# Router transposes in unused columns of score tiles, q's three pieces two steps each, ScalarE's, GpSimd's and the load jobs at other steps

## The chip, the cores and the metric

The kernel runs on one core of a Trainium2 chip. The core has five engines with in-order instruction queues: TensorE (matmuls and transposes, in the profile PE, with its weight loads as PEld), VectorE (DVE), ScalarE (ACT), GpSimd (POOL) and SyncE (SP), which here only issues DMAs. Matmul results land in PSUM, eight banks; everything else is in SBUF. The metric is the device time of one execution in microseconds, lower is better.

## What is computed

Sparse attention over 4 batch entries, 8 heads, 576 positions and head size 64, then a top-1 mixture of eight experts over the 2304 tokens, then one more layer for all tokens:

```python
scores = scale * q @ k.T                      # per batch entry and head, 576 x 576
thresh = max(scores) - tau
attn = softmax(where(scores >= thresh, scores, -1e9))
x = (attn @ v) -> (2304, 512)
logits = x @ w_gate                           # the router
e = argmax(logits); gate = softmax(logits)[e]
out = gate * (relu(x @ w1[e]) @ w2[e])
h = out @ w_in; result = (h - tanh(h)) @ w_out
```

All in float32 with the accuracy of float32: the kernel splits operands into a high and a low part and adds up several matmuls.

## The kernel before

**Attention stage.** `Attn.run` works through 16 units, which this text calls heads: unit u is head u % 8 of two batch entries at once (u // 8 chooses which two). Each has nine steps t = 0 to 8, one score tile of 128 rows by 576 columns each, so there are 144 steps. In step i the program emits the score matmuls of tile i + 2 (`scores`, L228), the row maximum of tile i + 1 (`smax`, VectorE, L236), its exponential (`sexp`, ScalarE, L242), and the mask of tile i (`smask`, VectorE, L255). A step ahead of all that and behind it has four phases, 0 to 3, in which further jobs stand; the queue of each engine is in the order of emission.

**The jobs of a head.** Their places are the table `PL`: step relative to the head's first step, and phase. A head's q and k are prepared some steps before: `dq` doubles q on GpSimd (`xq`, L129), `hi1` and `lo1` split k on ScalarE and GpSimd (L120, L124), `q0`, `m`, `q4` are q's three pieces of transposes on TensorE (L175; `m` holds one block of q and one of k), `k0`, `k5` those of k (L173). Each piece goes through one PSUM bank, tag "t", one buffer; it is evacuated by ScalarE (`eq0`, `em`, `eq4`, `ek0`, `ek5`; L197, L200, L204) and for q also by a VectorE subtraction for the low part (`fq0`, `fm`, `fq4`; L208), and the next piece has to wait for both. `vw`, `vh`, `vl` scale and split v (ScalarE L146, L150; GpSimd L154); `vm` are v's maxima for four heads (VectorE L132), done in four neighbouring steps of heads 3, 7 and 11.

Behind the mask, `se` casts the weights to 16 bits (ScalarE L263, tile e16, three buffers for groups of three steps), `sl` subtracts for the low part (GpSimd L267, L268, a large one for two steps and a small one for the third), `te` has SyncE issue a DMA transpose of a group (L273), which also frees its e16 buffer. The first three blocks of each group are transposed by TensorE instead into unused columns of a score tile (`tr_m`, L284, columns 288 to 480 of its first bank) and copied by ScalarE (`ev_m`, `et`, L287). `pv` multiplies with v (L311) into a bank that it shares with the router's logits; `po0` to `po2` read it on VectorE (L317), `st` stores.

**The router in the attention stage.** After each odd head the 512-wide rows of a head pair are ready. `lg_tr` transposes nine 128 x 128 blocks, in three groups, through the "t" bank (`lps`, L563), `lg_ev` copies each group on ScalarE (`xT`, L567), `lg_mm` multiplies with the router's weights (L571), `lg_add` adds to the logits on VectorE (L580). In `PL` these are `t0` to `t2`, `v0` to `v2`, `l0` to `l2` and `la`.

**Loads.** `lq`, `lk`, `lv` load q, k and v of four heads at once from SyncE's queue (L96 to L111), in which the DMA transposes and the stores stand too. q and k share one tag with three buffers.

**Expert layers.** After the last `lg_add` all tokens are routed, sorted by expert through indirect DMAs, and the expert layers and the last layer run.

The loop's core, in its order of emission:

```python
ps[i + 2] = self.scores(*steps[i + 2], ...)
nn[i + 1] = self.smax(ps[i + 1])
ee[i + 1] = self.sexp(ps[i + 1], nn[i + 1])
self.smask(*steps[i], ps.pop(i), nn.pop(i), ee.pop(i))
```

## Time and profile before

| | us |
|---|---|
| median of 3 runs | 1070.12 |
| lowest, highest | 1066.64, 1074.0 |
| the profiled execution, its own time | 1065.54 |
| its span, first to last instruction | 1063.8 |

Busy shares of that span: TensorE 88%, its weight loads 82%, VectorE 82%, ScalarE 68%, GpSimd 56%; mean granted TensorE clock 0.96. The attention stage takes about the first third of the span, the expert layers and the last layer the rest. A share is an average over these stages. In the rows below PE, PEld, DVE, ACT, POOL and SP are the engines, L an instruction's line in the kernel, `out<-in` its tiles. A row of waits says which engine and line stood for which, how long in total, how often, and the longest. Square brackets behind a row of the timeline are the idle time of that engine before the instruction and what ended it.

### The profile page before, as it was taken

To read this page: it belongs to the slowest core of one execution; us is meant where nothing else is said; L and a number is where in the kernel's file an instruction comes from. 1 tells how busy PE (TensorE), PEld (TensorE's weight loads), DVE (VectorE), ACT (ScalarE), POOL (GpSimd) and SP (SyncE) were. 2 spreads that over 40 slices of the span, in tenths; PEclk is the share of its full clock that TensorE was granted. 3 is DMA by queue.
4 is the path that set the end of the run, shared out by engine and by line. 5 is a ranking of instruction groups with operands and counts; after the bars stand their busy time and mean duration, and the time that the engine had idled before them with its cause. 6 is when DMAs were issued, how large, how long until landed. Compare 5 with 4: busy or idle time off the path is not lost.

```text
span 1063.8 us, 20919 instructions
## 1 busy us (share of the span) xinstructions
PE 940.9 (88%) x7441; PEld 869.2 (82%) x7441; DVE 872.7 (82%) x1667; ACT 721.4 (68%) x1359; POOL 597.0 (56%) x581
## 2 busy tenths in 40 slices
PE   4577787887787498999999998999999999999997
PEld 4466676776786398999999997889999999999986
DVE  5789979888985678786777787999989889898893
ACT  4698998897995175666676766666666566556662
POOL 2788877887876211120011027786867768677763
PEclk9699988998998599999999999999999999999999
DMA  5599999998979497786898875120101001000000
GB/s 138 106 194 170 174 184 180 173 188 182 147 142 170 119 311 251 252 264 223 273 307 279 281 255 171 46 77 21 48 1 42 26 21 48 1 30 1 21 11 31
DMA packets 230826, 147.85 MB, mean 139 GB/s; under 512 B 161306, under 2 KB 207660, under 8 KB 230717
## 3 DMA queue, kind: packets, MB, share of 16 engines
q1 hardware_dynamic: 226957, 135.68, 51.2%
q0 software_dynamic: 3312, 10.49, 3.1%
q8 instruction: 60, 0.98, 0.4%
q14 instruction: 49, 0.40, 0.1%
q10 hardware_dynamic: 448, 0.30, 0.1%
HBM read 85.08 MB, written 23.60 MB: 102 GB/s over the span
## 4 chain that ended last, share of the span: by engine, by line
PE 46%; DVE 10%; DMA 5%; ACT 2%; issue 2%; another core or an unknown queue 0%; SPq 0%; POOL 0%; POOLq 0%; DVEq 0%; ACTq 0%
PE h L1054 22%; PE y L1137 15%; PE y L1109 8%; DMA raw<-in_moe_w_dram 3%; DVE w L1255 2%; DVE w L1256 2%; DMA wscr<-cm 1%; DVE w L1024 1%; DVE w L1253 1%; DVE tm L1254 1%; DVE w L1257 1%; PE t L1031 1%; ACT w L1022 0%; DVE cm L1185 0%; DVE keep L584 0%
## 5 line engine op out<-in xcount | busy, mean ns | idle before, releaser
L267 POOL TENSOR_TENSOR e<-em,e 128x1024 f16<-128x1024 f32 (+1 forms) x98 | 158.1, 1614 | 61.1 <-issue 29.9
L1252 POOL TENSOR_SCALAR tm<-u 128x384 uint8<-128x384 f32 x88 | 128.9, 1465 | 50.2 <-ACT u L1248 49.6
L1054 PE MATMUL h<-xa,w 128*128 128x256 f32 (+6 forms) x864 | 139.3, 311 | 3.3 <-DVE hbuf L1090 1.3
L1109 PE MATMUL y<-hbuf,w 128*128 128x256 f32 (+6 forms) x864 | 139.8, 310 | 0.3 <-ACT yo L1112 0.2
L1054 PEld LDWEIGHTS h<-xa,w 128*128 128x128 f32 x864 | 129.7, 193 | 5.2 <-DVE hbuf L1090 1.8
L255 DVE SCALAR_TENSOR_TENSOR em<-sps,n,e 128x576 f32<-128x576 f32 x144 | 116.8, 811 | 15.8 <-ACT et L287 4.8
L1109 PEld LDWEIGHTS y<-hbuf,w 128*128 128x128 f32 x864 | 127.4, 190 | 1.2 <-ACT yo L1112 0.8
L1248 ACT ACTIVATE u<-h 128x384 f32<-128x384 f32 x96 | 47.1, 491 | 117.5 <-PE h L1054 117.5
L242 ACT ACTIVATE e<-sps,n 128x576 f32<-128x576 f32 x144 | 108.5, 754 | 26.3 <-DVE n L236 26.1
L1255 DVE SCALAR_TENSOR_TENSOR w<-y,w 128x384 f32<-128x384 f32 x96 | 122.5, 1276 | 0.0
L1071 POOL DMA_INDIRECT xr<-rows,idx x26 | 27.3, 1049 | 163.8 <-PE t L1031 158.8
L236 DVE TENSOR_REDUCE n<-sps 128x1 f32<-128x576 f32 x144 | 107.2, 744 | 11.1 <-PE sps L228 11.1
L311 PE MATMUL ops<-vh,et 128*128 128x64 f16 (+1 forms) x2240 | 94.9, 200 | 20.7 <-DVE x L317 20.7
L1054 PE MATMUL h<-xk,w 128*128 128x384 f32 x576 | 109.2, 337 | 2.0 <-DVE w L1024 1.7
L311 PEld LDWEIGHTS <-et 128*128 128x128 f16 (+1 forms) x2240 | 84.1, 106 | 31.1 <-issue 25.7
L1054 PEld LDWEIGHTS h<-xk,w 128*128 128x128 f32 x576 | 102.1, 188 | 6.7 <-DVE w L1024 2.4
L1269 POOL TENSOR_TENSOR gl<-w,gh 128x384 fp32r<-128x384 f32 x83 | 84.6, 1019 | 38.8 <-ACT gh L1268 38.8
L228 PE MATMUL sps<-ka,qa 128*128 128x288 f32 x320 | 84.5, 356 | 19.2 <-DVE n L246 9.1
L263 ACT CAST e<-em 128x576 f16<-128x576 f32 x144 | 98.8, 687 | 3.3 <-DMA et<-e 1.2
L1024 DVE TENSOR_TENSOR w<-raw,w 128x1024 fp32r<-128x1024 f32 x68 | 84.0, 1238 | 20.6 <-ACT w L1022 19.9
L1022 ACT CAST w<-raw 128x1024 fp32r<-128x1024 f32 x72 | 75.4, 1050 | 18.7 <-DVE free L611 11.9
L1256 DVE SCALAR_TENSOR_TENSOR w<-y,w 128x384 f32<-128x384 f32 x96 | 77.7, 809 | 10.0
(237 smaller groups left out, 2207.6 us busy)
## 6 DMA issues: line engine op xcount, KB each, us to landing
raw<-in_moe_w_dram SPq DMA_DIRECT2D x64, 512.0 KB
cv<-in_moe_w_in_dram SPq DMA_DIRECT2D x16, 512.0 KB
cv<-in_moe_w_out_dram SPq DMA_DIRECT2D x16, 512.0 KB
wscr<-cm SPq DMA_DIRECT2D x32, 256.0 KB
raw<-wscr SPq DMA_DIRECT2D x16, 512.0 KB
xw<-yT SPq DMA_DIRECT2D x24, 192.0 KB
vv<-in_v_dram SPq DMA_DIRECT2D x8, 512.0 KB
raw<-in_k_dram SPq DMA_DIRECT2D x6, 512.0 KB
```

Of the source, the lines that this page charges most:

```text
L236: nc.vector.tensor_reduce(out=n[:, 0:1], in_=ps[:, :, 0:288], axis=AX.XY, op=ALU.max, negate=True)
L242: nc.scalar.activation(out=e, in_=ps[:, :, 0:288], func=AF.Exp, bias=n[:, 0:1])
L255: nc.vector.scalar_tensor_tensor(out=self.em[u, g][:, i].rearrange("p (a b) -> p a b", a=2), in0=ps[:, :, 0:288], scalar=n[:, 1:2], in1=e, ...
L263: self.nc.scalar.copy(self.e16[u, g][:, i, 0:S], self.em[u, g][:, i])
L267: eng.tensor_tensor(out=e16[:, r, S + 64:], in0=em[:, r, 0:512], in1=e16[:, r, 0:512], op=ALU.subtract)
L311: nc.tensor.matmul(o[q], lhsT=et[:, base + c, q], rhs=vh[:, a, j, c if c < 5 else c - 5, :], start=(n == 0), stop=(n == len(terms) - 1))
L1054: self.nc.tensor.matmul(out, lhsT=a, rhs=b, start=(i == 0), stop=(i == len(parts) - 1))
L1109: nc.tensor.matmul(self.ys[d], lhsT=a[:, f % 2, s], rhs=b, start=(f == 0 and i == 0), stop=(f == 7 and i == 2))
L1137: nc.tensor.matmul(self.ys[m], lhsT=a[:, s], rhs=b[:, f % 2], start=(f == 0 and i == 0), stop=(f == 15 and i == 2))
L1252: nc.gpsimd.tensor_scalar(out=mk, in0=u, scalar1=RCUT * RCUT, scalar2=None, op0=ALU.is_gt)
L1255: V.scalar_tensor_tensor(out=w, in0=y, scalar=b, in1=w, op0=ALU.add, op1=ALU.mult)
L1256: V.scalar_tensor_tensor(out=w, in0=z, scalar=d, in1=w, op0=ALU.add, op1=ALU.mult)
```

## The change

The router's transposes of six of the eight head pairs (those of heads 1, 3, 5, 7, 9 and 11) no longer go through the "t" bank: a pair of blocks is transposed into columns 288 to 416 of the two banks of a score tile, ahead of its score matmuls (`lg_tr2`, at the steps `LGS`), and copied out by ScalarE right behind that tile's exponential (`lg_ev2`). Five copies take the place of three, and the small matmuls (`lg_mm2`) stand two steps after the transposes. The pairs of heads 13 and 15 keep the former way. In `PL` q's pieces and k's now stand at even distances of two steps and one or two for k, with ScalarE's evacuations at the head of the following step; `dq`, `hi1`, `lo1`, `vw`, `vh`, `vl` and the loads `lq` and `lv` stand at other steps. The first head's own table (`PFIRST`) and the last's (`PLAST`) stay.

```diff
--- before.py
+++ after.py
@@ -27,6 +27,7 @@
 RM = S - 512
 QS = S + 64
 MLAG = 3, 4
+LGS = 22, 23, 25, 26, 28
 
 
 class Attn:
@@ -208,11 +209,13 @@
         self.nc.vector.tensor_tensor(out=self.qview(self.QB[u % 2], what), in0=self.pview(pf, what),
                                      in1=self.qview(self.QA[u % 2].bitcast(F32), what), op=ALU.subtract)
 
-    def scores(self, u, t, m=None):
+    def scores(self, u, t, m=None, l=None):
         nc = self.nc
         ps = self.sp.tile([128, 2, 512], F32, tag="s", name="sps")
         if m:
             self.tr_m(ps, *m)
+        if l:
+            l[0].lg_tr2(ps, *l[1:])
         qa, qb, ka = self.QA[u % 2], self.QB[u % 2], self.ka[u]
         if t == 4:
             terms = [(j, 512 + 64 * j) for j in range(2)]
@@ -331,10 +334,10 @@
 
     LD = (6,)
 
-    PL = {"lq": (-21, 1), "lk": (-31, 2), "lv": (-12, 1), "dq": (-15, 1), "hi1": (-15, 3),
-          "lo1": (-13, 3), "q0": (-11, 1), "eq0": (-10, 1), "fq0": (-10, 2), "m": (-10, 2), "em": (-9, 1), "fm": (-9, 3), "q4": (-9, 3),
-          "eq4": (-8, 0), "fq4": (-8, 2), "k0": (-5, 0), "ek0": (-5, 0), "k5": (-5, 2), "ek5": (-4, 0),
-          "vm": (-7, 3), "vn": (-3, 1), "vc": (-3, 2), "vw": (4, 3), "vh": (5, 3), "vl": (6, 1),
+    PL = {"lq": (-25, 1), "lk": (-31, 2), "lv": (-18, 1), "dq": (-17, 1), "hi1": (-19, 1),
+          "lo1": (-14, 1), "q0": (-12, 1), "eq0": (-11, 0), "fq0": (-11, 2), "m": (-10, 1), "em": (-9, 0), "fm": (-9, 2), "q4": (-8, 1),
+          "eq4": (-7, 0), "fq4": (-7, 2), "k0": (-6, 1), "ek0": (-5, 0), "k5": (-5, 1), "ek5": (-4, 0),
+          "vm": (-7, 3), "vn": (-3, 1), "vc": (-3, 2), "vw": (3, 0), "vh": (6, 1), "vl": (7, 1),
           "se": (1, 2), "sl": (2, 0), "te": (4, 2), "pv": (11, 3), "po0": (14, 2),
           "po1": (20, 3), "po2": (20, 3), "de": (9, 3), "rc": (13, 1), "st": (32, 3), "t0": (23, 1), "v0": (24, 1), "l0": (31, 2),
           "t1": (24, 3), "v1": (24, 3), "l1": (28, 3), "t2": (29, 0), "v2": (29, 2), "l2": (30, 1), "la": (32, 2)}
@@ -355,7 +358,7 @@
     def run(self, units, moe=None):
         nc = self.nc
         NU = len(units)
-        sched = {}
+        sched, lgs = {}, {}
         PL = self.PL
         for x in self.AFTER:
             x, y = x.split()
@@ -402,7 +405,13 @@
             at(b, "de", self.denom, u)
             at(b, "rc", self.recip, u)
             at(b, "st", self.store, u)
-            if moe and u % 2 == 1:
+            if moe and u % 2 == 1 and b + LGS[-1] + 2 < 9 * NU:
+                P, j = u // H, u % H // 2
+                for x, i in enumerate(LGS):
+                    lgs[b + i] = moe, P, j, x
+                    sched.setdefault((b + i + 2, 3), []).append((moe.lg_mm2, (P, j, x)))
+                at(b, "la", moe.lg_add, P, j)
+            elif moe and u % 2 == 1:
                 P, j = u // H, u % H // 2
                 for g in range(3):
                     at(b, f"t{g}", moe.lg_tr, P, j, g)
@@ -419,12 +428,14 @@
                 f(*a)
             if 0 <= i + 2 < len(steps):
                 j = i - MLAG[0]
-                ps[i + 2] = self.scores(*steps[i + 2], (steps[j][0], steps[j][1] // 3) if j >= 0 and j % 3 == 0 else None)
+                ps[i + 2] = self.scores(*steps[i + 2], (steps[j][0], steps[j][1] // 3) if j >= 0 and j % 3 == 0 else None, lgs.get(i))
             for f, a in sched.get((i, 1), []):
                 f(*a)
             if 0 <= i + 1 < len(steps):
                 nn[i + 1] = self.smax(ps[i + 1])
                 ee[i + 1] = self.sexp(ps[i + 1], nn[i + 1])
+            if i - 1 in lgs:
+                moe.lg_ev2(ps[i + 1], *lgs[i - 1][1:])
             j = i - MLAG[1]
             if 0 <= j < len(steps) and j % 3 == 0:
                 if i + 2 - MLAG[1] + MLAG[0] >= len(steps):
@@ -485,7 +496,7 @@
     def __init__(self, tc, at, wg, w1, w2, w_in, w_out, out, rows, yT, cp, dp):
         self.tc, self.nc, self.attn, self.ident = tc, tc.nc, at, at.ident
         self.w1, self.w2, self.out, self.xtok, self.yT = w1, w2, out, rows, yT
-        self.cp, self.dp, self.xT, self.wgd = cp, dp, {}, wg
+        self.cp, self.dp, self.xT, self.xT2, self.wgd = cp, dp, {}, {}, wg
         nc = self.nc
         self.gscr = dp.tile([NTL, 128], F32, name="gscr")
         self.wscr = dp.tile([16, 128, 1024], F32, name="wscr")
@@ -565,6 +576,20 @@
     def lg_ev(self, P, j, g):
         self.xT[g] = self.attn.wk.tile([128, 3, 128], F32, tag="xT", name="xT", bufs=3)
         self.nc.scalar.copy(self.xT[g], self.lps[:, 0:3])
+
+    def lg_tr2(self, ps, P, j, x):
+        at = self.attn
+        for i in range(min(2, 9 - 2 * x)):
+            self.nc.tensor.transpose(ps[:, i, 288:416], at.X[4 * P + j][:, 2 * x + i], at.ident)
+
+    def lg_ev2(self, ps, P, j, x):
+        n = min(2, 9 - 2 * x)
+        self.xT2[x] = self.attn.wk.tile([128, 3, 128], F32, tag="xT", name="xT", bufs=3)
+        self.nc.scalar.copy(self.xT2[x][:, 0:n], ps[:, 0:n, 288:416])
+
+    def lg_mm2(self, P, j, x):
+        for i in range(min(2, 9 - 2 * x)):
+            self.nc.tensor.matmul(self.attn.lm[:, 2 * x + i], lhsT=self.xT2[x][:, i], rhs=self.wg[:, j], start=True, stop=True)
 
     def lg_mm(self, P, j, g):
         for i in range(3):
```

## Rows read from the trace of the kernel before

**Rows 1.** The page, first line: span and instructions.

```profile
span 1063.8 us, 20919 instructions
```

**Rows 2.** Timeline, VectorE: start us, duration, engine, line, operation, [idle before, releaser].

```profile
349.94 0.23 DVE L580 TENSOR_TENSOR L<-L,ops 128x72 f32<-128x72 f32 x1 [2.71 <-PE ops L571]
```

**Rows 3.** Busy time by head: length, engines, TensorE clock, DMA; last row fourteen heads.

```profile
78.97:100.00 21.03, 15.21 (x199) 13.61 (x200) 19.72 (x52) 18.38 (x35) 17.99 (x20) 0.92 0.97 181
100.00:117.84 17.84, 15.93 (x246) 14.96 (x244) 16.53 (x45) 16.55 (x30) 13.76 (x14) 1.00 0.69 109
117.84:139.64 21.80, 15.79 (x197) 14.26 (x198) 16.50 (x44) 18.92 (x35) 18.71 (x20) 0.84 1.05 219
157.47:180.30 22.83, 16.42 (x210) 14.74 (x211) 20.14 (x52) 17.98 (x34) 17.63 (x19) 0.85 1.03 196
198.12:219.68 21.56, 16.32 (x198) 14.83 (x198) 16.66 (x44) 18.50 (x35) 17.71 (x20) 0.84 1.11 223
237.50:260.56 23.06, 16.42 (x200) 14.78 (x200) 19.87 (x52) 18.12 (x34) 18.16 (x20) 0.85 0.93 194
278.38:298.28 19.90, 14.70 (x198) 13.35 (x198) 16.51 (x44) 18.41 (x35) 17.63 (x19) 0.91 0.98 176
42.52:316.11 273.59, 216.90 (x3020) 198.89 (x3019) 241.03 (x629) 243.15 (x438) 217.78 (x219) 0.93 0.93 172
```

**Rows 4.** Timeline of head 5, 131 to 136 us: ScalarE, TensorE, VectorE.

```profile
131.42 0.67 ACT L263 CAST e<-em 128x576 f16<-128x576 f32 x1 [0.99 <-POOL e L268]
132.00 0.82 ACT L146 ACTIVATE vv<-vv,sc 128x640 f32<-128x640 f32 x1
132.73 0.67 ACT L204 ACTIVATE ka<-tps,g 128x512 fp32r<-128x512 f32 x1
133.45 0.90 PE L563 MATMUL lps<-ident,x 128*128 128x128 f32 x3 [2.40 <-ACT ka L204]
134.12 0.82 DVE L255 SCALAR_TENSOR_TENSOR em<-sps,n,e 128x576 f32<-128x576 f32 x1 [1.77 <-issue]
135.18 0.83 PE L228 MATMUL sps<-ka,qa 128*128 128x288 f32 x2
```

**Rows 5.** Waits of VectorE, heads 1 to 14: us in total, times, longest.

```profile
DVE n L236 <- PE sps L228: 9.6, 14, 1.5
DVE em L255 <- ACT et L287: 4.8, 11, 0.8
DVE pm L132 <- DMA vv<-in_v_dram: 4.8, 3, 2.4
```

**Rows 6.** Waits of TensorE, heads 1 to 14.

```profile
PE tps L175 <- DVE qb L208: 19.3, 15, 1.6
PE ops L311 <- DVE x L317: 17.0, 21, 1.4
PE lps L563 <- ACT ka L204: 7.1, 6, 2.4
```

**Rows 7.** Groups by line and shape, heads 1 to 14: busy us, mean ns.

```profile
L287 ACT COPY et<-sps 128x384 f16<-128x384 f16 x41 | 19.8, 484 | 0.0
L567 ACT COPY xT<-lps 128x384 f32<-128x384 f32 x18 | 8.7, 486 | 1.7 <-PE lps L563 1.6
L200 ACT CAST qa<-tps 128x128 fp32r<-128x128 f32 x14 | 3.6, 259 | 0.0
L208 DVE TENSOR_TENSOR qb<-tps,qa 128x512 fp32r<-128x512 f32 x28 | 19.2, 685 | 1.3 <-ACT qa L200 0.6
L132 DVE TENSOR_REDUCE pm<-vv 128x1 f32<-128x640 f32 x12 | 9.7, 812 | 4.8 <-DMA vv<-in_v_dram 4.8
```

**Rows 8.** Waits of SyncE's DMA queue, heads 1 to 14.

```profile
SPq L273 <- POOL e L268: 78.6, 24, 6.6
```

**Rows 9.** Timeline of the start: first scores; doubling of head 1's q.

```profile
14.18 0.82 PE L228 MATMUL sps<-ka,qa 128*128 128x288 f32 x2 [2.80 <-DVE ka L202]
15.43 1.14 POOL L129 COPY xq<-raw 128x1152 f32<-128x1152 f32 x1 [12.83 <-DMA raw<-in_q_dram]
```

## The prediction

> **What bounds the kernel now.** The page gives the span [rows 1]: the profiled execution took 1065.54 us by its time, 1063.8 us of it from first to last instruction. The chain of waits that ended last can be followed back only into the expert layers, which the change leaves alone; there I looked for what they start from. In the timeline the last addition of router logits ends at 350.2 us, having waited for the router's last matmul [rows 2]. The routing takes a maximum over all those logits, so everything behind it moves one to one with that instruction. What the change can move is the attention stage ahead of it.
>
> There I cut the table of engine busy time by heads, from one head's first row maximum to the next one's [rows 3]. The pattern is the main finding. Even heads last 17.84 us at a granted clock of 1.00 (heads 4, 6, 8, 10, 12 and 14 are alike within 0.02 us). Odd heads, which do the same nine steps, last 19.90 to 23.06 us at 0.84 to 0.92. Fourteen heads take 273.59 us. VectorE is busy 16.5 us in an even head and in a plain odd one (5, 9, 13); in heads 3, 7 and 11, which carry the four v maxima, 19.7 to 20.1.
>
> What is different in an odd head shows in the timeline of head 5 [rows 4]. TensorE stood 2.40 us before the router's transposes `lps`: they want the one "t" bank, which still holds a k piece, and its evacuation `ka` (L204, 132.73) stands on ScalarE behind a late cast (0.99 us) and v's scaling (L146, 132.00). The exponential is queued behind these, and the mask starts at 134.12 after 1.77 us of idle VectorE. The scores, in order behind `lps`, come only at 135.18, and their pair of matmuls takes 0.83 us. The waits over the 14 heads fit: VectorE 9.6 us for scores, 4.8 for v's load in three waits, 4.8 for the `et` copy [rows 5]; TensorE 7.1 us at `lps`, 19.3 for the evacuation of q's low parts, 17.0 for the `x` outputs [rows 6].
>
> **The change part by part.** *Router transposes in score tiles.* Six of the eight head pairs no longer take the "t" bank. Transposes and small matmuls stay nine each per pair, so TensorE gains no work; the place in the queue changes: a pair of transposes now stands directly before a tile's score matmuls, where they wait for nothing but the slot that the scores need as well. The 7.1 us wait and what hangs on it go. The evacuation becomes five copies instead of three. Three were 0.486 us each for 384 columns; a 128-column cast from the "t" bank takes 0.259 [rows 7], so I put 256 columns between, at 0.37. In the six pairs that is 24 x 0.37 + 6 x 0.26 = 10.4 us against 18 x 0.486 = 8.7: 1.7 us more on ScalarE over 14 heads, 0.1 us a head.
>
> More than their length counts where they stand: right behind the exponential, and the mask of that tile reads the same banks. Today the mask waits for the `et` copy out of its own tile in 11 cases, 4.8 us together, 0.44 each [rows 5]; there are 41 such copies in the stretch [rows 7], so about one in four holds it. The Trainium skill, page "PSUM — Partial Sum Buffer", section "PSUM bank collisions raise a hardware error", says that two engines are to be kept apart on one bank, two reads of different columns included. The trace agrees (those 11 waits); by the page the 30 new copies are all ahead of their masks, and if unused columns were really free, this term would be 0. Price from the rows: nothing if ScalarE is always early, 30 x 0.37 = 11 us if it is always late; I take one in four at 0.44: 3.0 us, nearest to the `et` rows.
>
> *q's pieces two steps apart.* Now the middle piece's transposes are queued directly behind the VectorE subtraction that frees their bank, once a head, and this is the 19.3 us [rows 6]. With a step between, the subtraction is done when TensorE gets there. TensorE is not the bound in even heads (clock 1.00, VectorE's wait for scores is small), so most of it is hidden anyway. What comes late instead: q4's subtraction now stands in the same step directly before the two `x` outputs, whose bank TensorE wants; its wait of up to 1.4 us there [rows 6] grows by about one subtraction of 512 columns, 0.685 us [rows 7]. The next scores have a step's lead, which covers that; without cover it would be 14 x 0.7 = 10 us.
>
> *ScalarE and GpSimd dealt out.* v's scaling moves from beside the two k evacuations to a step of its own, the cast of v's high part and k's split likewise. In an even head VectorE is idle 17.84 - 16.53 = 1.3 us [rows 3], and such a clump of scaling and evacuation is one cause; I take back 0.3 (bounds 0 and 1.3). On GpSimd each group of a large and a small subtraction now gets one extra job behind the small one, so the DMA transpose that SyncE issues no longer waits for it; SyncE stood 78.6 us for these subtractions [rows 8]. This costs nothing where ScalarE's next cast into the same e16 slot is still later; where it is not, I read the 0.99 us before a cast [rows 4] as such a case: the row names the subtraction that ended last, but the slot is freed only by the DMA transpose of three groups before.
>
> *Loads.* q is asked for four steps, v six steps earlier: about 8 and 12 us. The 4.8 us of v waits [rows 5] go. The q load now waits for the doubling of the last head of its group, one step before it, with DMA transposes queued behind it on SyncE; the doubling is a GpSimd copy of 1.14 us [rows 9], done while SyncE is busy with the transpose ahead; without that cover it costs SyncE 3 x 1.14 = 3.4 us, at worst all of it time.
>
> *Start.* Head 1's first q piece now stands before the first scores. They start at 14.18 us, but the doubled q is there only at 15.43 + 1.14 = 16.57 [rows 9]: up to 2.4 us plus the transposes' own. The first exponential already stands behind that piece's evacuation on ScalarE, so the mask hardly moves: between 0 and 3, I take 0.5.
>
> **The sum.** Base for a head without v maxima: 17.84 - 0.3 = 17.5. Plain odd heads: (21.80 - 17.5) + (21.56 - 17.5) + (19.90 - 17.5) = 10.8. Heads 3, 7, 11: VectorE's own work, 16.53 + 4 x 0.812 [rows 3, 7] = 19.8: 1.2 + 3.0 + 3.3 = 7.5. Even heads: 6 x 0.3 = 1.8. Together 20.1; less 3.0 for the copies and 0.5 for the start: 16.6, say 17 us. Check from below: ScalarE is busy 243.15 us in these 273.59 [rows 3], with the longer copies 244.9; so no more than 28 us can go. Against the profiled execution's own 1065.5 this is 1048.5. The runs shown have a median of 1070.1, 4.6 us above it; new runs will lie between these scales, and I forecast **1051 us**.
>
> **Rivals.** *The copies hold the masks, and ScalarE is late in odd heads* (0.18). ScalarE is busy 18.92 us in head 5 against 16.55 in head 4 [rows 3], though the code gives only two copies more, 0.97 us. If that is real work, plain odd heads stay near 18.9 and lose 3 x 1.4 = 4 us, and the copies rise towards their 11. Gain 5 to 13; at 9 it is 1059. For it: the mask's waits for `et`. Against it: the rest of the 18.92 is likely instructions that no longer overlap in a stalled queue.
>
> *The DMA transposes become the bound, no change* (0.07). Heads that follow faster ask for their e16 slots sooner. The 0.99 us wait of a cast [rows 4] would have to come 17 times, somewhat more than once a head, to eat the gain: 1068. For it: SyncE's long waits, and transposes, loads and stores on one queue. Against it: ScalarE shows such a wait in few places, and the small subtractions come sooner.
>
> *TensorE's clock, slower* (0.07). Odd heads run at 0.84 to 0.92, and in head 5 a 2.40 us stand comes before scores that take 0.83 us [rows 3, 4]. The place is the wait for the `x` outputs: 1.4 us today, 2.1 with the subtraction before it, in every head; it decides if even heads fall below 1.00 as well. Then they last like heads 13 and 5, 2.1 to 4.0 us longer: 6 x 3 = 18 us, and the odd ones gain nothing: 1065.5 + 18 = 1083. Against it: the waits at q's middle piece and at `lps` go, and each even head has had a wait of this kind at 1.00. The Trainium skill, page "TensorE: Matmul & The Clock Gate", section "A second HAM failure mode: psum-queue depth-cycling", says that short idles between groups of matmuls that cycle through PSUM can make the clock oscillate; by it the slower case would be the rule here. The even heads' 1.00 does not agree.
>
> *More than forecast* (0.06): the even heads too come down to ScalarE's floor, gain 25 to 28, 1040.
>
> **How the numbers follow.** Forecast 0.62 with 1043 to 1057: the even heads' term between 0 and 1.3 a head, the copies between 0 and 6, the start up to 3. Taking in most of the first rival, the range is 1041 to 1063; the slower case, no change and the larger gain stay outside with 0.20. A change of 1%, 10.7 us, is about what a measurement of this kernel can tell from none. Faster by more: 0.62 + 0.06 + half the first rival = 0.77; within 1%: 0.09 + 0.07 = 0.16; slower 0.07.
>
> **What would show it.** Right: odd heads without v maxima at 17.4 to 18.0 us and clock 1.00, heads 3, 7, 11 near 19.8; no wait at `lps` before head 13's; no VectorE wait for v's load; the wait for q's low part gone; the mask's wait for the router copies a few us; the last logit addition at about 333. Wrong: new waits of a mask for `xT` over 8 us, casts waiting for the DMA transposes, even heads below clock 1.00, or later layers that take longer than before.

## The result and the profile after

The changed kernel takes 1056.37 us (median of 4 runs, 1053.64 to 1057.43), the kernel before beside it 1070.86: a ratio of 0.987 with a 95% interval of 0.984 to 0.990, 14.5 us less. The forecast was 1051, its range 1041 to 1063. The profiled execution took 1053.64 us, 11.9 less than the 1065.54 of before, with this span on the page:

```profile
span 1051.9 us, 20946 instructions
```

The last addition of router logits ends 13.5 us sooner than before [rows 2]. Timeline of the changed kernel, VectorE:

```profile
336.46 0.23 DVE L605 TENSOR_TENSOR L<-L,ops 128x72 f32<-128x72 f32 x1 [2.71 <-PE ops L596]
```

Busy time by head of the changed kernel, columns as in [rows 3]: heads 2 to 5, 7, 10, 12 and 13, and the fourteen heads:

```profile
58.81:78.92 20.11, 15.27 (x203) 14.32 (x202) 16.45 (x44) 16.98 (x32) 17.24 (x19) 0.83 1.12 215
78.92:100.61 21.69, 16.59 (x219) 15.22 (x215) 19.91 (x52) 18.33 (x34) 17.92 (x19) 0.92 0.88 147
100.61:117.22 16.61, 14.74 (x238) 14.11 (x238) 16.43 (x44) 16.47 (x33) 13.63 (x15) 1.00 0.78 128
117.22:136.13 18.91, 15.66 (x227) 14.43 (x226) 16.41 (x44) 17.19 (x34) 16.14 (x17) 1.00 1.09 230
...
155.35:175.65 20.30, 15.28 (x221) 13.84 (x218) 19.85 (x52) 17.86 (x33) 16.99 (x19) 1.00 1.01 184
...
210.22:229.60 19.38, 15.21 (x211) 14.16 (x211) 16.57 (x45) 17.65 (x35) 15.89 (x17) 0.91 1.12 221
...
250.25:266.88 16.63, 14.55 (x237) 13.92 (x237) 16.38 (x45) 16.63 (x33) 14.27 (x15) 1.00 0.79 125
266.88:284.06 17.18, 14.38 (x222) 13.58 (x221) 16.42 (x45) 17.10 (x34) 16.14 (x17) 1.00 1.03 191
...
42.03:299.88 257.85, 209.97 (x3012) 196.03 (x3013) 239.40 (x628) 240.58 (x448) 217.78 (x219) 0.95 0.97 181
```

The fourteen heads lost 15.7 us. Where: heads 5, 9 and 13 together 9.2 (63.3 to 54.0 us), heads 3, 7 and 11 4.3, the even heads 4, 8, 12 and 14 5.6, head 1 1.0. Heads 2, 6 and 10 grew by 4.3 (18.71, 17.83, 17.82 to 20.11, 19.22, 19.38), which no term of the forecast's sum had. Head 12 is the picture of a head at its floor: 16.63 us long, VectorE busy 16.38 and ScalarE 16.63 of it.

Waits of the changed kernel over the same heads (columns as in [rows 5]):

```profile
PE ops L314 <- DVE x L320: 35.4, 27, 3.7
...
ACT e L266 <- DMA et<-e: 9.5, 9, 2.2
...
DVE n L239 <- PE sps L231: 3.8, 6, 1.0
...
DVE em L258 <- ACT xT L588: 1.8, 5, 0.4
...
PE tps L176 <- DVE qb L209: 0.4, 1, 0.4
```

TensorE's wait for q's low part went from 19.3 us to 0.4, that for the `x` outputs doubled from 17.0 to 35.4 [rows 6], VectorE's for scores fell from 9.6 to 3.8 [rows 5], and the waits at `lps` and for v's load are gone. New is ScalarE's: casts wait 9.5 us for DMA transposes in nine waits, in the kernel before 1.0 in two, or 2.0 with the one that its profile puts down to GpSimd [rows 4].

Outside the fourteen heads, head 1 begins 0.5 us sooner (42.03 us instead of 42.52), the part from the last row maximum to the last logit addition takes 23.48 us instead of 20.40, and all behind it 715.44 instead of 713.86. The other profiles have 713.94 to 716.11 for that last part, and 713.94 and 716.11 are two executions of one program (e3, e3b), so its 1.6 us tell nothing.

### The profile page after: what moved, and what is told of

Same layout as the page of the kernel before. It is cut to its first block, busy times and chain, and to the rows that moved or that the text cites. A ratio compares the mean times of both kernels' runs of the same rounds, so it can differ in the third digit from the quotient of the medians.

```text
span 1051.9 us, 20946 instructions
## 1 busy us (share of the span) xinstructions
PE 933.8 (89%) x7441; PEld 866.5 (82%) x7441; DVE 872.8 (83%) x1667; ACT 719.2 (68%) x1371; POOL 596.9 (57%) x581
## 4 chain that ended last, share of the span: by engine, by line
PE 47%; DVE 10%; DMA 4%; issue 3%; ACT 3%; POOL 0%; SPq 0%; POOLq 0%; DVEq 0%; another core or an unknown queue 0%; ACTq 0%
PE h L1079 23%; PE y L1162 15%; PE y L1134 8%; DVE w L1280 2%; DVE w L1281 2%; DMA raw<-in_moe_w_dram 1%; DVE w L1049 1%; DMA xr<-rows,idx 1%; DVE w L1278 1%; DMA cv<-in_moe_w_in_dram 1%; ACT w L1047 1%; DVE tm L1279 1%; PE t L1056 1%; DVE w L1282 1%; DMA wscr<-cm 1%
## 5 line engine op out<-in xcount | busy, mean ns | idle before, releaser
L245 ACT ACTIVATE e<-sps,n 128x576 f32<-128x576 f32 x144 | 110.7, 769 | 15.5 <-DVE n L239 14.9
L266 ACT CAST e<-em 128x576 f16<-128x576 f32 x144 | 101.1, 703 | 12.3 <-DMA et<-e 9.5
L1049 DVE TENSOR_TENSOR w<-raw,w 128x1024 fp32r<-128x1024 f32 x68 | 84.1, 1238 | 20.2 <-ACT w L1047 20.0
L1047 ACT CAST w<-raw 128x1024 fp32r<-128x1024 f32 x72 | 75.4, 1051 | 17.9 <-DVE free L636 12.0
```

The costliest lines, as they stand in the source:

```text
L245: nc.scalar.activation(out=e, in_=ps[:, :, 0:288], func=AF.Exp, bias=n[:, 0:1])
L266: self.nc.scalar.copy(self.e16[u, g][:, i, 0:S], self.em[u, g][:, i])
```

## The experiments

Each run is read by its time in the fourteen heads of its profile, since the rest of the program is the same. What the runs hold, and the result; the whole time is the median of as many runs as the brackets say:

| run | router in tiles | q and k spaced | jobs dealt out | q, v load at | fourteen heads, us | whole time, us (runs) |
|---|---|---|---|---|---|---|
| before | | | | -21, -12 | 273.59 | 1070.86 (4) |
| e1 | x | | | -21, -12 | 272.10 | 1066.50 (1) |
| e9 | | | v's scaling alone | -21, -12 | 265.04 | 1061.19 (1) |
| e5, e5b | | | x | -21, -12 | 260.11, 262.98 | 1054.58 (1), 1055.38 (4) |
| e8 | x | | x | -25, -18 | 273.77 | 1068.17 (1) |
| e2 | x | x | | -25, -18 | 263.40 | 1060.28 (1) |
| after; e4 | x | x | x | -25, -18 | 257.85; 260.27 | 1056.37 (4); 1057.27 (1) |
| e6; e7 | x | x | x | -21, -18 | 259.72; 263.88 | 1059.13 (8); 1060.10 (10) |
| e3, e3b | x | x | x | -21, -12 | 256.84, 257.43 | 1051.23 (1), 1053.96 (4) |
| e10 | x | x | x | -21, -14 | 251.90 | 1048.31 (4) |

The kernel before took 1062.62 us in the one run beside e1 to e4, 1067.28 (median of 17) beside e5 to e8, and 1069.51 (of 7) beside e9, e10, e3b and e5b.

e5 and e5b are one program, as are e3 and e3b, and e4 differs from the changed kernel only behind these heads. The pairs are 2.9, 0.6 and 2.4 us apart, so differences of less than 3 us between two profiles tell nothing by themselves; a single head differs by up to 2.4 us between two executions of one program (head 5: 18.35 in e3, 20.79 in e3b). q's spacing without the router in the score tiles was not tried: by the order of emission the router's transposes and q's pieces would then wait for each other at the "t" bank.

### The router alone (e1_router_alone)

```diff
 # the changed kernel, with the whole table PL of the kernel before
-    PL = {"lq": (-25, 1), ..., "vl": (7, 1), ...}
+    PL = {"lq": (-21, 1), ..., "vl": (6, 1), ...}
```

> The kernel before with only the router's transposes moved into the score tiles; all other jobs and loads stand where they stood. Measured from the first row maximum of head 1 to that of head 15 (273.59 us before, 257.85 after the whole change) and by head. Theory (the wait for the t bank makes the odd heads long): heads 5, 9 and 13 fall from 21.8, 21.6, 19.9 to about 18 us, heads 3, 7, 11 by under 1 us each since v's load still comes late there, even heads stay at 17.8; the fourteen heads take about 263. Rival (ScalarE's clump of v's scaling and k's evacuation makes them long, the bank only shows it): odd heads fall by less than 1 us each, fourteen heads above 270.

Busy time by head of this run, heads 5 and 7 and the fourteen:

```profile
117.73:137.19 19.46, 14.23 (x201) 12.95 (x202) 16.42 (x44) 17.38 (x33) 16.12 (x18) 0.97 1.06 226
...
155.71:180.05 24.34, 15.59 (x205) 14.28 (x206) 20.51 (x52) 17.63 (x34) 17.66 (x19) 0.93 0.96 184
...
41.49:313.59 272.10, 211.43 (x3020) 193.96 (x3019) 243.02 (x628) 242.21 (x450) 218.17 (x219) 0.95 0.95 173
```

The plain odd heads do fall (head 5 from 21.80 to 19.46, head 9 from 21.56 to 19.94, head 13 from 19.90 to 18.40), 5.5 us together, but head 7 rises from 22.83 to 24.34, and heads 3, 7 and 11 and the even heads together give back 4.0. In all it is 1.5 us, half of what two executions of one program differ by, and the whole time, 1066.50 us, is not below the 1062.62 of the kernel before beside it. So neither theory fits whole: the plain odd heads fall by more than the rival allowed, the stage as little as it said. Taking the router off the t bank, on which most of the forecast's sum stood, gives nothing measurable by itself.

### The jobs back at their old steps (e2_jobs_back)

```diff
 # the changed kernel
-  "dq": (-17, 1), "hi1": (-19, 1), "lo1": (-14, 1), "vw": (3, 0), "vh": (6, 1), "vl": (7, 1)
+  "dq": (-15, 1), "hi1": (-15, 3), "lo1": (-13, 3), "vw": (4, 3), "vh": (5, 3), "vl": (6, 1)
```

> The changed kernel with the six jobs of ScalarE and GpSimd (q's doubling, k's split, v's scaling, cast and low part) back at their places of before; router, q's pieces and loads as changed. Heads 4, 8 and 12 take 16.63 us after the change and took 17.82 before. Theory (dealing out the jobs is what took 1.2 us from these heads): they go back to 17.3 us or more. Rival (q's pieces two steps apart did it): they stay at 16.6 to 16.9.

Busy time by head of this run, head 4 (heads 8 and 12 are within 0.01 us of it):

```profile
100.86:118.75 17.89, 14.93 (x223) 13.74 (x222) 16.56 (x45) 16.75 (x33) 14.33 (x16) 1.00 0.83 119
```

Without the dealt-out jobs the even heads are back at 17.9 us, as in the kernel before, and the fourteen take 263.40. The jobs give heads 4, 8 and 12 their whole 1.27 us, where the forecast took 0.3.

### The jobs alone (e5_jobs_alone, e5b_jobs_alone_timed)

```diff
 # the kernel before
-  "dq": (-15, 1), "hi1": (-15, 3), "lo1": (-13, 3), "vw": (4, 3), "vh": (5, 3), "vl": (6, 1)
+  "dq": (-17, 1), "hi1": (-19, 1), "lo1": (-14, 1), "vw": (3, 0), "vh": (6, 1), "vl": (7, 1)
```

> The kernel before, with only the jobs dq, hi1, lo1, vw, vh and vl at the changed kernel's steps; the router goes through the t bank, q's pieces and the loads stand as before. In the changed kernel these places were worth 5.5 us (fourteen heads 263.4 us with the jobs at their old steps, 257.85 with all of the change). Theory A, the parts add up, because what the jobs remove is a queue on ScalarE and GpSimd that has nothing to do with the t bank: fourteen heads 273.6 - 5.5 = about 268, heads 4, 8 and 12 at 16.6 to 16.9. Theory B, the jobs pay only once TensorE comes to its scores in time: heads 4, 8 and 12 stay above 17.5 and fourteen heads above 271, since VectorE's wait for scores (9.6 us in 14 waits in the kernel before) remains what ends its idle time.

> The jobs alone (dq, hi1, lo1, vw, vh, vl at the changed kernel's steps, all else as before) once more, timed in rounds. Theory A, what the single look said: fourteen heads near 260, ratio to the kernel before 0.987 to 0.990, the same as all of the change, which would mean that router, q's spacing and loads together add nothing measurable to the jobs. Theory B, the look was a favourable run: ratio 0.991 to 0.996, and the rest of the change gives a third to two thirds of its gain.

Busy time by head of the first of the two, heads 4, 5 and 9 and the fourteen:

```profile
97.71:114.82 17.11, 15.24 (x231) 14.40 (x230) 16.44 (x45) 16.41 (x30) 13.28 (x13) 1.00 0.72 135
114.82:132.91 18.09, 13.90 (x212) 12.26 (x210) 16.64 (x44) 17.24 (x33) 16.32 (x19) 1.00 1.06 219
...
190.72:208.63 17.91, 13.89 (x212) 12.25 (x210) 16.64 (x44) 17.24 (x33) 16.32 (x19) 1.00 1.12 225
...
40.82:300.93 260.11, 208.30 (x3016) 190.20 (x3016) 240.99 (x628) 241.31 (x438) 217.73 (x219) 0.97 0.96 180
```

Six entries of the table, with the t bank, q's pieces and the loads untouched, take 13.5 us out of the fourteen heads in one execution and 10.6 in the other. In four timed runs they give 1055.38 us against 1069.51, a ratio of 0.9856 (0.983 to 0.988): within the intervals the same as all of the change. Neither theory of the first run had it: the jobs are worth more alone than as the last part of the change, 5.5 us. The parts do not add up, they overlap: the router alone gives 1.5, the jobs alone 10.6 to 13.5, both with q's spacing 16.2 to 16.8 (e3b, e3). By whole time the router and the spacing together add nothing measurable to the jobs: 1053.96 us (e3b) against 1055.38.

### v's scaling alone (e9_v_scaling_alone)

```diff
 # the kernel before
-  "vw": (4, 3)
+  "vw": (3, 0)
```

> The kernel before, with v's scaling (vw) alone moved from phase 3 of step 4 to phase 0 of step 3. The run with all six jobs moved took 13.5 us out of the fourteen heads (273.6 to 260.1) without any other part of the change. Theory A: the scaling is the cause, since it stands on ScalarE just ahead of the k evacuation for which the router's transposes wait at the t bank (2.40 us in head 5): fourteen heads at 260 to 264, TensorE's wait at lps down to 4 us or less, heads 5, 9 and 13 at 18 to 18.5. Theory B: the jobs on GpSimd and k's split count as well, since in the kernel before three of them follow one another within four phases and the small subtractions, the DMA transposes and the masks come late: the scaling alone gives 3 to 7 us, fourteen heads at 266 to 271.

Busy time by head of this run, heads 4 and 5:

```profile
97.68:114.81 17.13, 15.13 (x230) 14.29 (x229) 16.43 (x46) 16.77 (x32) 14.14 (x15) 1.00 0.67 109
114.81:136.45 21.64, 15.36 (x214) 13.87 (x213) 16.50 (x44) 18.71 (x35) 17.75 (x20) 0.92 1.09 216
```

One entry of the table gives 8.6 us, and by neither theory's road. The even heads gain 0.7 each, head 2 1.7, head 13 1.7 and head 3 1.2, but heads 5 and 9 stay at 21.64 and 21.46. Timeline of this run at the end of head 5, the place of [rows 4]:

```profile
120.74 0.95 SPq L330 DMA_DIRECT2D rows<-x  x1
121.86 13.51 SPq L273 DMA_TRANSPOSE et<-e  x3
...
129.92 0.67 ACT L263 CAST e<-em 128x576 f16<-128x576 f32 x1 [2.51 <-DMA et<-e]
130.50 0.68 ACT L204 ACTIVATE ka<-tps,g 128x512 fp32r<-128x512 f32 x1
...
131.23 0.58 PE L563 MATMUL lps<-ident,x 128*128 128x128 f32 x3 [3.20 <-ACT ka L204]
...
131.90 0.82 DVE L255 SCALAR_TENSOR_TENSOR em<-sps,n,e 128x576 f32<-128x576 f32 x1 [2.57 <-issue]
```

The scaling is no longer between the cast and `ka`, and the stall is longer than before. What stands at its head is the cast, and now the row names what it waits for: a DMA transpose, which SyncE issued at 121.86 behind the k load and the stores. In the kernel before the same transpose was issued at 124.59 and the cast went at 131.42 [rows 4], 6.83 us later; here it is 8.06. The row of before named GpSimd's subtraction, which ended at the same moment. In this run `lps` and the t bank only pass the wait on: TensorE still waits 7.3 us there over the heads (7.1 before), and the stage is 8.6 us shorter. In the first run with all six jobs the same cast waits 0.70 us, and SyncE issues that transpose 5.6 us into the head instead of 7.0. That the small subtractions, which stand earlier on GpSimd there, do this is argued from the order of the queues and not shown. Nor does the earlier issue settle it: in the second execution of the same program (e5b) the transpose is issued 5.8 us into the head, and the cast goes 7.98 us later, not 7.37, waits 1.42 us, and head 5 takes 20.16 us. How long the transpose itself takes counts as well: in e9 one of this head's three lands 8.0 us after its issue, the others 5.5 and 5.7. That the loads and stores ahead of it lengthen it is likely and not shown.

### q's pieces back (e8_q_back)

```diff
 # the changed kernel
-  "q0": (-12, 1), "eq0": (-11, 0), "fq0": (-11, 2), "m": (-10, 1), ..., "q4": (-8, 1), ..., "k0": (-6, 1), ..., "k5": (-5, 1)
+  "q0": (-11, 1), "eq0": (-10, 1), "fq0": (-10, 2), "m": (-10, 2), ..., "q4": (-9, 3), ..., "k0": (-5, 0), ..., "k5": (-5, 2)
```

> The changed kernel with q's and k's pieces (q0 to fq4, k0 to ek5) at the steps of the kernel before; router in the score tiles, jobs and loads as changed. From the other runs the spacing seems to be worth 8 to 10 us (272.1 us for fourteen heads with the router alone, 263.4 with the spacing and the loads added, of which the loads gave nothing). Theory A: fourteen heads at 266 to 268, TensorE's wait for q's low part back at 17 to 20 us, the even heads 0.5 to 1 us longer. Theory B, what I had forecast, that most of that wait is hidden: fourteen heads at 258 to 260 although the wait is back.

The edit puts back k's pieces with q's, so what follows is the spacing of both. The fourteen heads take 273.77 us, the whole gain lost, more than either theory allowed. But it is lost in three heads: heads 3, 7 and 11 take 27.14, 27.40 and 25.97 us, 17.9 more than in the changed kernel, while heads 8 and 12 take 17.0, 0.4 more (head 4, behind the first of the long ones, 1.2). Timeline of this run in head 3:

```profile
80.13 0.67 ACT L266 CAST e<-em 128x576 f16<-128x576 f32 x1 [3.79 <-DMA et<-e]
...
81.32 0.69 DVE L209 TENSOR_TENSOR qb<-tps,qa 128x512 fp32r<-128x512 f32 x1 [3.99 <-ACT qa L201]
81.93 0.75 DVE L239 TENSOR_REDUCE n<-sps 128x1 f32<-128x576 f32 x1
...
82.07 0.47 PE L176 MATMUL tps<-ident,xq 128*128 128x128 f32 x1 [5.29 <-DVE qb L209]
```

A cast waits 3.79 us for a DMA transpose; the evacuation of q's first piece stands behind it on ScalarE, the subtraction waits for that on VectorE, with the next row maximum behind it, and q's middle piece for the subtraction on TensorE, with the next scores behind it. GpSimd's next subtraction, which needs the cast, waits 4.31 us. One late transpose stops four engines. With a step between the pieces such a delay costs less: in e6 a cast of head 7 waits 3.64 us, and the head takes 24.25 us and not 27.40. So the spacing is worth 0.4 us a head where nothing is late and up to 7 where a load delays a transpose. What router and jobs give together without q's spacing and with the loads as before is left open: no run had that.

### The loads (e3_loads_back, e3b_loads_back_timed, e6_q_load_back, e7_k_load_apart, e10_v_load_behind)

```diff
 # the changed kernel
-  "lq": (-25, 1), "lk": (-31, 2), "lv": (-18, 1)
+  "lq": (-21, 1), "lk": (-31, 2), "lv": (-12, 1)     # e3, e3b
+  "lq": (-21, 1), "lk": (-31, 2), "lv": (-18, 1)     # e6
+  "lq": (-21, 1), "lk": (-33, 2), "lv": (-18, 1)     # e7
+  "lq": (-21, 1), "lk": (-31, 2), "lv": (-14, 3)     # e10
```

> The changed kernel with the loads of q and v back at their steps of before. Heads 2, 6 and 10 take 20.1, 19.2 and 19.4 us after the change (18.7, 17.8, 17.8 before), with a cast that waits 1.4 us or more for a DMA transpose. Theory (q's load, asked for one DMA transpose earlier, holds that transpose): heads 2, 6, 10 fall to 17 to 18 us, the casts' waits for DMA transposes fall from 9.5 us in the fourteen heads to under 5, and v's late load costs heads 7 and 11 up to 2.4 us each again. Rival (the queue of DMAs is simply full at this pace): the casts wait 8 us or more for DMA transposes all the same, in other heads.

> The changed kernel with both loads at the steps of the kernel before (q -21, v -12), once more, timed in rounds. Theory A: the loads' new steps give nothing (what the v waits lose, the DMA transposes gain): ratio to the kernel before 0.984 to 0.988, equal to or 1 to 3 us below the changed kernel. Theory B: the looks favour it by chance, and the v waits (5.4 us in two) cost more in most executions: ratio 0.990 or more.

> The changed kernel with q asked for at step -21, as in the kernel before; v's load stays at the new step -18. In the run with both loads put back, heads 2, 6 and 10 lost 1.2 us or more each and heads 7 and 11 gained 2.2 each. Theory A, two separate causes (the q load ahead of a DMA transpose in SyncE's queue, and v's late arrival): heads 2, 6 and 10 at 17.7 to 18.9, heads 7 and 11 at 20.2 to 20.7, fourteen heads 253 to 254, time 1052 to 1053 where the changed kernel has 1056.4. Theory B, the DMA queue is full in these heads whatever the order: the q load at the later step delays other transposes together with v's load, which now follows more closely, so that heads 3, 7 and 11 grow by what 2, 6 and 10 lose: fourteen heads 256 to 258, time 1055 to 1057.

> The run with the q load back at step -21 and, in addition, the k load two steps earlier (step -33 instead of -31), so that it no longer stands directly beside the stores in SyncE's queue with a transpose behind both. Theory A: the pair of k load and stores is what delays the transpose at which casts wait 0.7 to 1.6 us near the ends of heads 5 and 9; these two heads lose about 1 us each, the casts' wait for DMA transposes falls by 2 to 3 us, fourteen heads 2 us below the run without it, time about 1050. Theory B: a load costs a transpose its time wherever it stands, the wait moves to the head before: no difference over 0.5 us.

> As the run with both loads put back, but v's load asked for at step -14, phase 3: directly behind a DMA transpose in SyncE's queue, with three steps to the next one, where the other places stand less than two steps ahead of one. Theory A: what a load costs depends on how soon a transpose follows it; here v comes some 3 us earlier, its wait (2.8 us in heads 7 and 11) goes or shrinks below 1, casts do not wait longer than 5 us in all, heads 7 and 11 at 20 to 20.7: fourteen heads at 252 to 253, 4 us below the run with the loads put back. Theory B: the DMA engines have about 250 us of work in this stage whatever the order, so the transposes of head 3, 7 and 11 come later by what v comes earlier: fourteen heads at 256 to 259.

With both loads back (e3) heads 2, 6 and 10 are shorter by 1.2 to 1.5 us each, heads 7 and 11 longer by 2.1 to 2.2 (in e3b heads 2 and 6 are shorter by 1.7 and 2.4, head 10 longer by 0.7, heads 7 and 11 longer by 1.8 and 1.5); the timed ratio is 0.9843 (0.981 to 0.988), which overlaps with the changed kernel's. The change's new places for the loads give nothing that can be measured: the v wait that goes (5.4 us in e3, 4.4 in e3b) comes back as casts that wait for DMA transposes (9.5 us instead of 5.2 and 7.0). How a load costs is seen in SyncE's queue. In the second of these runs (e3b) v's six DMAs are issued, and four transposes directly behind them:

```profile
229.34 0.62 SPq L110 DMA_DIRECT2D vv<-in_v_dram  x1
...
232.31 1.25 SPq L112 DMA_DIRECT2D vv<-in_v_dram  x2
233.73 19.35 SPq L276 DMA_TRANSPOSE et<-e  x4
...
237.61 0.82 DVE L133 TENSOR_REDUCE pm<-vv 128x1 f32<-128x640 f32 x1 [2.25 <-DMA vv<-in_v_dram]
```

With q at its old place and v's at -18 (e6) the two loads follow each other by three steps, and the theory of two separate causes falls: heads 2, 6 and 10 get shorter as it said (18.46, 17.17, 18.97), but heads 3, 7 and 11 grow to 23.07, 24.25 and 21.93, more than the rival said. Timeline of that run at the start of head 7:

```profile
156.16 0.41 PE L314 MATMUL ops<-vh,et 128*128 128x64 f16 x8 [2.77 <-DMA et<-e]
156.48 0.67 ACT L266 CAST e<-em 128x576 f16<-128x576 f32 x1 [3.64 <-DMA et<-e]
```

Its ratio is 0.9915 (0.989 to 0.994). With k's load two steps earlier as well (e7) nothing is gained: 0.9935 (0.991 to 0.996).

In e10 v's DMAs stand directly behind a transpose, with the stores and then the next transpose after them. Timeline of SyncE in that run, at the end of head 6 and the start of head 7:

```profile
146.85 3.73 SPq L276 DMA_TRANSPOSE et<-e  x1
150.62 0.59 SPq L110 DMA_DIRECT2D vv<-in_v_dram  x1
...
157.86 17.06 SPq L276 DMA_TRANSPOSE et<-e  x4
```

Busy time by head of the same run, heads 7 and 11 and the fourteen:

```profile
151.35:171.77 20.42, 15.09 (x221) 13.58 (x220) 20.23 (x51) 17.97 (x35) 17.40 (x19) 1.00 1.06 215
...
224.09:244.32 20.23, 14.94 (x216) 13.48 (x215) 20.06 (x51) 18.03 (x35) 17.42 (x19) 1.00 1.11 202
...
42.06:293.96 251.90, 207.12 (x3014) 191.96 (x3013) 240.22 (x628) 239.28 (x448) 217.73 (x219) 0.97 1.00 185
```

Heads 7 and 11 come to VectorE's own 20.2 and 20.1 us of work, v's wait is 0.2 us in all, the casts wait 5.6. Against e3, which differs in v's place alone, 4.6 of the 4.9 us come from these two heads. The four runs have a median of 1048.31 us against 1069.51, a ratio of 0.9802 (0.977 to 0.983): the fastest of all, 5.7 us below e3b beside it, whose four runs do not reach down to these (1047.65 to 1051.42 against 1052.44 to 1056.5), and ahead of both kernels. It was not put together with other places for q's load or k's.

### The last head (e4_last_head)

```diff
 # the changed kernel, the last head's own table
-    PLAST = {"te": (4, 3), ...
+    PLAST = {"vw": (4, 3), "vh": (5, 3), "vl": (6, 1), "te": (4, 3), ...
```

> The changed kernel with v's scaling, cast and low part at their places of before in the last head alone. After the change VectorE's two subtractions at the end of the attention stage take 1.41 and 1.17 us beside GpSimd's work on v's low part, where they took 0.69 and 0.22 before, and the stage's tail from the last row maximum to the last logit addition is 23.7 us against 20.6. Theory (two engines hold each other up there): they take 0.69 and 0.22 again and the tail shrinks by 1.7 to 3 us. Rival (the tail is long for TensorE's lower clock there, whatever VectorE does): it shrinks by less than 1 us.

From the last row maximum to the last logit addition this run takes 24.5 us, the changed kernel 23.48, the kernel before 20.40. The jobs of the last head are not the cause. e4 does not prove it by itself, since VectorE's two subtractions still take 0.90 and 1.17 us in it; but with all jobs back (e2) they take 0.69 and 0.22 as in the kernel before, and the tail is 23.2 us. The router alone has 23.5 too, and v's scaling alone 24.6. Busy time of that part and of a stretch in the middle of it, first in the kernel before, then in the changed kernel:

```profile
329.54:349.94 20.40, 16.61 (x278) 15.05 (x278) 5.16 (x16) 7.30 (x15) 7.09 (x12) 0.83 0.88 171
336.00:345.00 9.00, 6.84 (x116) 6.22 (x117) 1.19 (x5) 0.96 (x2) 1.51 (x5) 0.81 0.98 188
```

```profile
312.98:336.46 23.48, 17.35 (x278) 15.76 (x276) 6.84 (x16) 6.81 (x14) 7.81 (x13) 0.78 0.79 146
320.00:331.00 11.00, 8.58 (x104) 7.96 (x105) 1.19 (x5) 1.57 (x4) 1.82 (x5) 0.53 0.73 141
```

TensorE's granted clock is 0.53, near the lower of its two levels (1.2 of 2.4 GHz), where it was 0.81, and six of the router's small matmuls take 1.43 us instead of 0.81. All profiles but the one of before have this tail (23.2 to 24.8 us), whatever they change, also e1 and e8, whose stage is about as long as before. That speaks for a lucky profile of the kernel before, which at 1065.54 us is also 5.3 below that kernel's median; one profile of it cannot show it.

## Why the prediction came out right, and where its steps did not

The time was forecast within 6 us, and the sum of the steps in the heads within 1.4: 17.1 us there and 0.5 lost at the start, against 15.7 and 0.5 gained. Behind the heads the tail took 3.1 us more, which no step had, so the last logit addition came 13.5 us sooner and not 16.6, at 336.5 us and not at 333. That the heads' sum is right is luck in good part, because errors met: too much was put down to the t bank, too little to the jobs, and nothing to what the loads cost heads 2, 6 and 10.

**The base of the even heads: too small a term.** "I take back 0.3 (bounds 0 and 1.3)": heads 4, 8 and 12 came down by 1.2, to 16.6. The jobs do it (e2: back to 17.9), 0.7 of it by v's scaling alone (e9: 17.13). The upper bound was the right value; nearly all of VectorE's idle time in an even head [rows 3] went.

**Plain odd heads: right in size, the cause half told.** Forecast -10.8, measured -9.2. The step that failed reads [rows 4] as one stall at the t bank. In these three heads the router alone took 5.5 us, but the jobs alone took 10.0 and 7.1 with the bank as it was, and over the fourteen heads the router gave 1.5 and the jobs 10.6 to 13.5. Two stalls of VectorE follow each other there: 1.77 us before the mask, whose exponential stands behind the cast and `ka` on ScalarE, and 1.45 us before the next row maximum, whose scores stand behind `lps`. Timeline at the end of head 5, the second stall in the kernel before:

```profile
136.52 0.76 DVE L236 TENSOR_REDUCE n<-sps 128x1 f32<-128x576 f32 x1 [1.45 <-PE sps L228]
```

The same place with the router alone (e1), ScalarE and VectorE:

```profile
131.32 0.67 ACT L266 CAST e<-em 128x576 f16<-128x576 f32 x1 [0.98 <-POOL e L271]
134.28 0.82 DVE L258 SCALAR_TENSOR_TENSOR em<-sps,n,e 128x576 f32<-128x576 f32 x1 [2.02 <-issue]
```

The stall at the bank is gone, the one at the cast stays. The prediction's rows were read up to `ka` and the scaling, and the 0.99 us before the cast was told but not priced. e9 shows what stands at the head of that first stall: a transpose late in SyncE's queue, a cast that waits for its slot, and `ka`, exponential and mask behind it. How much of an odd head it is stays open: in the changed kernel the cast waits 1.64 us, longer than before, and head 5 is 2.9 us shorter all the same.

**GpSimd's jobs at nothing.** "This costs nothing where ScalarE's next cast into the same e16 slot is still later" was weighed only for a cost. As a gain it is part of what the jobs give beyond the scaling (265.0 to 260.1 and 263.0 us; the second difference is within the spread of two executions, so its size stays open). The row on which the step stood measures it badly: SyncE's wait named for the small subtractions fell from 78.6 us [rows 8] to 14.8, but the waits named for q's doubling rose from 10.9 to 40.1 and those for v's split from 6.0 to 33.6, since now these are what ended last.

**Heads 3, 7 and 11.** Forecast 19.8, measured 21.69, 20.30 and 20.65. VectorE's work in them was right (19.85 to 19.91 us busy). They are 1.8, 0.5 and 0.8 us longer than that work, and in them casts wait 1.3, 0.6 and 0.9 us for DMA transposes. How much of that the loads cause is not shown: with q's load back and v's at the better place of e10 the heads take 20.80, 20.42 and 20.23.

**Loads.** "The 4.8 us of v waits [rows 5] go": they went, and gave nothing that can be measured, since casts now wait for the transposes behind the loads. The rival of the DMA transposes had 0.07 and was thought of in every head, with some 17 us of casts' waits; it came in part, with 9.5 us in nine waits, 4.4 us of it in heads 2, 6 and 10, and cost the 4.3 us by which these grew: with q's load back they are shorter (e3, e6). The 3.4 us bound for the doubling of q was not needed: the q load waited 0.2 us.

**q's pieces.** The wait went from 19.3 us to 0.4. The one at the `x` outputs grew by 18.4 us where some 10 were forecast, and the scores' lead covered it: VectorE's wait for scores fell from 9.6 us to 3.8. "most of it is hidden anyway" holds in plain heads (e8: 0.4 us) and not where a transpose is late.

**The copies.** 3.0 us forecast, 1.8 measured, in 5 masks of 30, although the copies were longer than put down (0.392 us for 256 columns, 0.319 for 128). The masks' waits for the `et` copies, which no step touched, fell from 4.8 us to 0.2, so both kinds together cost less than before. The copied columns are read by no mask. The Trainium skill, page "PSUM — Partial Sum Buffer", section "PSUM bank collisions raise a hardware error", says that two engines must be kept apart on one bank even on disjoint columns; the five waits agree.

**Start.** 0.5 us lost was forecast, 0.5 gained was measured. The first mask did come 0.9 us later (20.59 us, not 19.66), within the bounds; by the third (23.83, not 23.90) that was made up.

**The slower rival.** TensorE's clock did not fall in the even heads without loads: it is 1.00, the upper of its two levels, in heads 4, 8, 12 and 14. It is 0.83 in head 2 and 0.91 in heads 6 and 10, where casts wait for transposes behind q's load; with the loads back it is 1.00 in all three in e3 and in two of them in e3b (0.91 in head 10), although the wait for the `x` outputs is there as well, 29.7 us in 27 waits in e3.

## What to carry to other kernels

When several stalls stand in a row, go back to the first instruction that was late and ask what frees its buffer; the releaser that the profile names may only have ended at the same time, and a fix further down the chain leaves the first wait in place, as e1 did here. In one in-order DMA queue a load can be paid by the transfer behind it: in this kernel it did best right behind an urgent one, and not right ahead of the next (e10 against e3). Try the cheap reordering alone before adding a new data path, because it may hold all of the gain.

## What the runs showed of the hardware

A VectorE subtraction and GpSimd's hold each other up. In the kernel before, the two subtractions of the last head that VectorE does took 0.69 and 0.22 us, in a pause of GpSimd's. Timeline of e3, VectorE and GpSimd at the same place:

```profile
313.74 1.42 POOL L155 TENSOR_TENSOR vh<-vv,vh 128x640 f16<-128x640 f32 x1
314.06 3.02 DVE L270 TENSOR_TENSOR e<-em,e 128x512 f16<-128x512 f32 x1 [1.49 <-ACT e L266]
...
315.09 1.17 POOL L270 TENSOR_TENSOR e<-em,e 128x512 f16<-128x512 f32 x1
316.21 0.33 POOL L271 TENSOR_TENSOR e<-em,e 128x64 f16<-128x64 f32 x1
```

The same instruction took 3.02 us and ended 0.54 us after GpSimd's run of three did. In the changed kernel it took 1.41 us, and a GpSimd subtraction beside it 1.60 instead of 1.16. The Trainium skill, page "SBUF — State Buffer", section "Who interferes with whom", says that a VectorE instruction with two SBUF inputs contends with a GpSimd instruction that reads SBUF, over a pair of ports that is an exclusive lock. The trace agrees. The masks, which read one operand from PSUM, do not show it: the 126 of the fourteen heads take 0.811 us in the mean, before and after, with GpSimd busy 217.78 us of that time.

The DMA engines have about the same work in every run: share times length of the fourteen heads is 254 us before, 250 after and 252 in e10, where the share is 1.00. Single heads show more than 1.00 (1.18 in head 6 of e10), so this is no exact bound, but a further gain in this stage would have to look at the transfers first.
